# A new step table for a retention + FFN kernel: first group in half-tiles, dummy matmuls at the opening, weights no longer gated

## The chip, the cores and the metric

The kernel runs on one NeuronCore of a Trainium2 chip. The metric is the device time of one execution in microseconds (us). Thirteen executions of the kernel before are shown; one more execution of it was recorded by the hardware profiler, and every duration below is read from that record.

The core has a matmul engine (PE, with its weight loads listed apart as PEld), three engines for elementwise work (DVE, ACT, POOL), a queue engine (SP) that here only issues DMAs, and 16 DMA engines that move data between HBM and on-chip memory. Matmuls write to PSUM, eight banks of 128 x 512 float32. POOL does not touch PSUM in this kernel.

## The reference

```python
scores = q @ k.T / sqrt(64)                    # 8 batches, 8 heads, 576 positions, head width 64
Dmat   = where(rel >= 0, gamma[h] ** rel, 0)   # decay by distance, causal; gamma[h] = 1 - 2**(-5-h)
x      = (scores * Dmat) @ v                   # -> 4608 tokens x 512
h      = x @ w_in                              # 512 x 2048
g      = where(h > 0, h, exp(min(h, 0)) - 1)   # ELU
out    = g @ w_out                             # 2048 x 512, float32
```

Inputs and output are float32; the kernel multiplies in bfloat16.

## The kernel before

The work has two halves that run interleaved. **Attention** is cut into 40 *units*: five for each batch, of which four cover 256 positions of four heads (unit `u` has `T = (u % 5) // 2`, the 256 positions, and `w = u % 5 % 2`, the heads), and the fifth is a short tail of 64 positions and all heads. The decay is folded into q and k, so that a running state per head carries what lies before a chunk of 128 positions. **FFN** is cut into 9 *groups* of 512 tokens. Group 0 is batch 0's first 512 tokens, that is units 0 and 1 (tokens 0 to 255) and 2 and 3 (256 to 511). Group 1 holds unit 4 (the tail of batch 0, 64 tokens), units 5 and 6 (256 tokens), and three quarters of units 7 and 8.

Nothing is left to a scheduler. A string `PLAN` lists some 1550 steps; the kernel walks it once, each step emits its instructions, and every instruction is pinned, so each engine executes its own steps in exactly the order of the table and waits where data or a buffer is not there. The steps, with the line that their instructions carry in the profile:

- `ld.u.q/k/v` load 256 KB of float32 (L323; tails L319 and L315), issued on SP. Each DMA on SP waits for the completion of the one eight places before it. Nine buffers take q and k of a unit together (`rqk`), eight take v (`rv`), two take a tail's.
- `wi.n`, `wo.n` load a quarter of w_in or w_out with a cast to bfloat16 (L286; 1 MB read, 512 KB written), issued on POOL, in POOL's order.
- `ca.u.q/k/v.e` cast and scale q, k (L354, tails L350) or cast v (L211), on engine `e`: `v` is DVE, `s` ACT, `p` POOL. `tr` transposes four 128 x 128 pieces on PE (L374), `tc` copies them out of PSUM (L211); `dt` does the same by a DMA transpose on SP (L367).
- `st` state products, `sc` scores, `in` the part that comes from the running state, `va` scores times v, all on PE (L203, output names `x` and `sc`); `mk` applies the mask on DVE (L449, L452); `pm`, `pe` add up the state on DVE (L211, L536, L542); `dm`, `de` spread it into a block diagonal (L545); `ou` copies the result out of PSUM into the group's `xt` tile (L211).
- `f.g.ft.lo.n.nf.tag` is the first FFN product (L203, output `ph`): hidden tiles `ft` to `ft+nf-1` (128 hidden values each) of group `g`, tokens `lo` to `lo+n`, into PSUM bank `tag`. It needs quarter `ft // 4` of w_in. `ex` is the exponential on ACT (L585). Then either `re...s`, a relu in place on ACT (L591), or `re...v`, a subtraction of 1 on DVE that writes a tile called `em` (L594); `el` joins the two into `g` on DVE (L603 or L605).
- `a.g.it.m.tag` is a quarter `m` of the second product for 128 tokens (L203, output `pm`): it needs quarter `m` of w_out. `y` copies the sum out (L211), `so` stores it (L624, on POOL; the last four on SP).
- `wm.n.tag`: `n` matmuls of zeros, 128 x 512. The code is there and the table does not use it.

A step written `x>y` also waits until `y` has been completed: a *gate*. The table before has two: `wi.0>ld.2.v` and `ld.4.q>wo.1`.

The table before does units 0 to 3 first, then all sixteen hidden tiles of group 0 at 512 tokens, then the second product of group 0 with units 4 to 8 between its quarters, then group 1, whose first product is split into 320 tokens (units 4, 5, 6) and 192 tokens (units 7, 8). From group 2 on, first and second products of neighbouring groups alternate with attention between them.

Of the kernel before, what the change touches and what calls it, by code (L numbers as in the profile page):

```python
# [16 lines left out]
PAIRS = {('st', 0): ('pm', 'h2'), ('st', 1): ('pm', 'h2'), ('st', 2): ('pm', 'h2'), ('st', 3): ('h1', 'h2')}  # L17
STATE_PAIR = {0: ('st', 0), 1: ('st', 1), 2: ('st', 2), 3: ('st', 3)}
OUT_PAIR = {(3, 0): ('st', 3), (3, 1): 4, (4, 0): 6}
SCORE_PAIR = {4: 5}  # L20
PLAN = """
ld.0.q ld.0.k ld.0.v ld.1.q ld.1.k ld.1.v ca.0.q.v ld.2.q tr.0.q.h0 ld.2.k ca.0.k.p tc.0.q.v ld.2.v ca.0.v.s ld.3.q.0
tr.0.k.h1 tc.0.k.s ld.3.k.0 st.0 ca.1.q.v sc.0 ld.3.v.0 pm.0 mk.0 tr.1.q.h0 ld.3.q.1 dm.0.p ld.3.k.1 ca.1.k.p in.0
pe.0 ca.1.v.s ld.3.v.1 tc.1.q.v va.0 de.0.p ou.0.1.s tr.1.k.h1 ou.0.0.s ca.2.q.v st.1 tc.1.k.s pm.1 tr.2.q.h0 pe.1
dm.1.p sc.1 tc.2.q.v de.1.p mk.1 in.1 ca.2.v.s wi.0>ld.2.v ca.3.q.v.0 ca.2.k.p va.1 ca.3.v.s.0 ou.1.1.s ca.3.q.v.1
wi.1 ou.1.0.s tr.2.k.h1 st.2 tc.2.k.s ca.3.k.p.0 pm.2 ca.3.v.s.1 pe.2 ca.3.k.p.1 sc.2 tr.3.0.h0 mk.2 wi.2 st.3.0
st.3.1 tc.3.0.s dm.2.p tr.3.1.h0 pm.3 sc.3.0 va.2 de.2.p tc.3.1.s pe.3 mk.3.0 in.2 dm.3.p ou.2.0.s sc.3.1 va.3.0
mk.3.1 ou.2.1.s wi.3 in.3.0 in.3.1 ou.3.0.s.0 de.3.p ou.3.1.s.0 va.3.1 ou.3.1.s.1 wo.0 ou.3.0.s.1 f.0.0.0.512.1.h0
wo.1 f.0.1.0.512.1.h1 wo.2 ex.0.0.0 wo.3 re.0.0.0.v f.0.2.0.512.1.pm ex.0.1.0 el.0.0.0 re.0.1.0.s f.0.3.0.512.1.x0
ex.0.2.0 el.0.1.0 f.0.4.0.512.1.h2 ex.0.3.0 re.0.2.0.v re.0.3.0.s f.0.5.0.512.1.x1 el.0.2.0 ex.0.4.0 el.0.3.0  # L30
f.0.6.0.512.1.h0 ex.0.5.0 re.0.4.0.v re.0.5.0.s f.0.7.0.512.1.h1 el.0.4.0 ex.0.6.0 f.0.8.0.512.1.pm el.0.5.0 ex.0.7.0
re.0.6.0.v re.0.7.0.s f.0.9.0.512.1.x0 el.0.6.0 ex.0.8.0 f.0.10.0.512.1.h2 el.0.7.0 ex.0.9.0 re.0.8.0.v re.0.9.0.s
f.0.11.0.512.1.x1 ex.0.10.0 el.0.8.0 f.0.12.0.512.1.h0 ex.0.11.0 el.0.9.0 ld.4.q>wo.1 re.0.11.0.s f.0.13.0.512.1.h1
re.0.10.0.v ld.4.k ex.0.12.0 el.0.11.0 f.0.14.0.512.1.pm ld.4.v ex.0.13.0 el.0.10.0 re.0.13.0.s f.0.15.0.512.1.x0
re.0.12.0.v ld.5.q ex.0.14.0 el.0.13.0 a.0.1.0.h2 ld.5.k ex.0.15.0 el.0.12.0 ld.5.v ca.4.q.p re.0.15.0.s a.0.2.0.h1
re.0.14.0.v ld.6.q el.0.15.0 a.0.1.1 ld.6.k el.0.14.0 ca.4.k.p ld.6.v a.0.2.1 tr.4.q.h0 a.0.0.0.pm ld.7.q ca.4.v.p
tc.4.q.v a.0.1.2 a.0.0.1 ld.7.k ca.5.q.v a.0.2.2 ld.7.v ca.5.k.p tr.5.q.h0 a.0.0.2 tc.5.q.v ld.8.q ca.5.v.s tr.5.k.h0
a.0.1.3 ld.8.k ca.6.q.v tc.5.k.s tr.6.q.h0 ld.8.v y.0.1 ca.6.k.p sc.5 tc.6.q.v sc.4 st.5 mk.5 a.0.0.3 ld.9.q ca.6.v.s
so.0.1.p tr.6.k.h2 pm.5 ld.9.k y.0.0 a.0.2.3 mk.4 dm.5.p tc.6.k.s pe.5 ca.7.q.v a.0.3.0.pm ld.9.v so.0.0.p y.0.2
de.5.p in.5 ca.7.v.s in.4 ld.10.q ca.7.k.p sc.6 va.5 va.4 mk.6 st.6 ou.5.1.s tr.7.q.h0 a.0.3.1 so.0.2.p ou.5.0.s  # L40
ld.10.k ou.4.0.s pm.6 ou.4.1.s tc.7.q.v tr.7.k.h2 dm.6.p a.0.3.2 ca.8.q.v tc.7.k.s ld.10.v pe.6 ca.8.k.p tr.8.q.h1
in.6 tc.8.q.v va.6 ld.11.q a.0.3.3 ca.8.v.s de.6.p ou.6.1.s ou.6.0.s sc.7 st.7 y.0.3 mk.7 ld.11.k tr.8.k.h0 ca.9.q.p
f.1.0.0.320.1.h2 tc.8.k.s so.0.3.p ld.11.v f.1.1.0.320.1.h1 ex.1.0.0 pm.7 ca.9.k.p f.1.2.0.320.1.h0 pe.7 ld.12.q
ex.1.1.0 re.1.0.0.v dm.7.p re.1.1.0.s el.1.0.0 ex.1.2.0 ca.9.v.p dt.9 el.1.1.0 f.1.3.0.320.1.h2 de.7.p re.1.2.0.v
f.1.4.0.320.1.h1 ca.10.q.v ex.1.3.0 ca.10.k.p ld.12.k re.1.3.0.s el.1.2.0 ex.1.4.0 el.1.3.0 f.1.5.0.320.1.h0
re.1.4.0.v dt.10 ca.10.v.s f.1.6.0.320.1.h2 el.1.4.0 ex.1.5.0 a.1.0.0.pm ex.1.6.0 ca.11.q.v re.1.5.0.s ld.12.v
f.1.7.0.320.1.h1 re.1.6.0.v ld.13.q el.1.5.0 ca.11.k.p ex.1.7.0 el.1.6.0 f.1.8.0.320.1.h0 re.1.7.0.s ld.13.k
f.1.9.0.320.1.h2 ca.11.v.s el.1.7.0 ex.1.8.0 dt.11 f.1.10.0.320.1.h1 ca.12.q.v ex.1.9.0 a.1.0.1 re.1.8.0.v re.1.9.0.s
ex.1.10.0 el.1.8.0 ld.13.v in.7 el.1.9.0 ca.12.k.p sc.8 ld.14.q sc.9 re.1.10.0.v va.7 st.8 mk.8 ou.7.0.s
f.1.11.0.320.1.h0 ou.7.1.s f.1.12.0.320.1.h2 dt.12 ex.1.11.0 el.1.10.0 ca.12.v.s mk.9 f.1.13.0.320.1.h1 re.1.11.0.s  # L50
pm.8 ld.14.k ex.1.12.0 ca.13.q.v dm.8.p ex.1.13.0 ld.14.v el.1.11.0 re.1.13.0.s ca.13.k.p pe.8 f.1.14.0.320.1.h0
re.1.12.0.v el.1.13.0 ld.15.q a.1.0.2 ex.1.14.0 de.8.p el.1.12.0 re.1.14.0.v dt.13 f.1.15.0.320.1.h1 el.1.14.0
# [12 lines left out]
ca.19.q.p pm.15 ou.14.1.s f.2.0.0.512.1.h1 pe.15 dm.15.p ld.21.q f.2.1.0.512.1.h2 ca.19.k.p ex.2.0.0 ld.21.k de.15.p
re.2.0.0.v in.15 ex.2.1.0 sc.16 ca.19.v.p va.15 el.2.0.0 dt.19 st.16 re.2.1.0.s f.2.2.0.512.1.h0 mk.16 ou.15.0.s
ou.15.1.s f.2.3.0.512.1.h1 ld.21.v ca.20.q.p ex.2.2.0 pm.16 el.2.1.0 a.1.3.1 ld.22.q ex.2.3.0 dm.16.p pe.16 re.2.2.0.v
re.2.3.0.s ca.20.k.p f.2.4.0.512.1.h2 ld.22.k el.2.2.0 in.16 de.16.p el.2.3.0 ex.2.4.0 sc.17 va.16 ca.20.v.p st.17
mk.17 dt.20 ou.16.0.s f.2.5.0.512.1.h0 ou.16.1.s ca.21.q.p f.2.6.0.512.1.h1 re.2.4.0.v ex.2.5.0 ld.22.v pm.17
ca.21.k.p el.2.4.0 re.2.5.0.s a.1.3.2 ld.23.q ex.2.6.0 pe.17 ld.23.k el.2.5.0 dm.17.p f.2.7.0.512.1.h2 dt.21 de.17.p  # L70
re.2.6.0.v in.17 ca.21.v.p ex.2.7.0 el.2.6.0 sc.18 sc.19 va.17 ld.23.v st.18 ca.22.q.p re.2.7.0.s mk.18
f.2.8.0.512.1.h0 ou.17.1.s ld.24.q ou.17.0.s ca.22.k.p f.2.9.0.512.1.h1 mk.19 ex.2.8.0 pm.18 el.2.7.0 ld.24.k a.1.3.3
dm.18.p ex.2.9.0 re.2.8.0.v dt.22 ca.22.v.p re.2.9.0.s f.2.10.0.512.1.h2 pe.18 el.2.8.0 y.1.3 de.18.p el.2.9.0 ld.24.v
f.2.11.0.512.1.h0 ex.2.10.0 ca.23.q.p re.2.10.0.v in.18 in.19 ex.2.11.0 so.1.3.p ld.25.q sc.20 el.2.10.0 va.18
ca.23.k.p va.19 re.2.11.0.s st.20 mk.20 ld.25.k f.2.12.0.512.1.h1 ou.18.0.s ou.18.1.s ld.25.v ca.23.v.p
f.2.13.0.512.1.h2 ou.19.0.s pm.20 ou.19.1.s dt.23 el.2.11.0 ex.2.12.0 ca.24.q.p a.2.0.0.pm pe.20 ex.2.13.0 dm.20.p
re.2.12.0.v de.20.p ld.26.q re.2.13.0.s f.2.14.0.512.1.h0 el.2.12.0 ca.24.k.p el.2.13.0 f.2.15.0.512.1.h1 ex.2.14.0
dt.24 re.2.14.0.v f.3.0.0.512.1.h2 ex.2.15.0 ca.24.v.p el.2.14.0 re.2.15.0.s a.2.0.1 ld.26.k ca.25.q.p ex.3.0.0
el.2.15.0 f.3.1.0.512.1.h0 ld.26.v re.3.0.0.v ca.25.k.p ld.27.q f.3.2.0.512.1.h1 el.3.0.0 ex.3.1.0 ld.27.k ca.25.v.p
# [75 lines left out]
def kernel(  # L155
# [213 lines left out]
    def turn(u, part, tag):  # L369
        u = int(u)  # L370
        ptr[u, part] = p = psum[tag].tile([P, 4, P], BF16, name="ptr", tag=tag)
        for j in range(4):
            lo = (2 * j + int(part) if part in "01" else "qk".index(part) * 4 + j) * P
            last = pin(nc.tensor.transpose(p[:, j], flat(u)[:, lo : lo + P], ident))  # L374
# [33 lines left out]
    def state_pair(u):  # L408
        return STATE_PAIR.get(u, u)
# [266 lines left out]
```

## Time and profile before

| | us |
|---|---|
| median of 13 executions | 322.34 |
| lowest, highest | 320.97, 324.96 |
| the profiled execution, own time | 321.5 |
| its span, first to last instruction | 319.6 |

| engine | busy us | share of the span |
|---|---|---|
| PE | 297.6 | 93% |
| PEld | 154.6 | 48% |
| DVE | 208.4 | 65% |
| ACT | 181.8 | 57% |
| POOL | 146.2 | 46% |

A matmul counts as busy from its start until its result is out, about 0.38 us for 512 columns, while the next one starts 0.216 us after it (four in 0.86 us on the chain of waits): PE's busy share is therefore no share of its peak. In the lists, "x16" is a count, "mean ns" the mean length of one instruction, and "idle before" the time in which the engine stood still ahead of that group, with what ended the wait. "L203" and "L211" are helpers that many steps share, so the tile names tell them apart. The granted clock is the share of full speed that the throttle let PE have, as the record has it.

### The profile page before, as it was taken

To read this page: it belongs to the slowest core of one execution; us is meant where nothing else is said; L and a number is where in the kernel's file an instruction comes from. 1 tells how busy PE (TensorE), PEld (TensorE's weight loads), DVE (VectorE), ACT (ScalarE), POOL (GpSimd) and SP (SyncE) were. 2 spreads that over 40 slices of the span, in tenths; PEclk is the share of its full clock that TensorE was granted. 3 is DMA by queue.
4 is the path that set the end of the run, shared out by engine and by line. 5 is a ranking of instruction groups with operands and counts; after the bars stand their busy time and mean duration, and the time that the engine had idled before them with its cause. 6 is when DMAs were issued, how large, how long until landed. Compare 5 with 4: busy or idle time off the path is not lost.

```text
span 319.6 us, 7795 instructions
## 1 busy us (share of the span) xinstructions
PE 297.6 (93%) x3076; PEld 154.6 (48%) x3076; DVE 208.4 (65%) x387; ACT 181.8 (57%) x380; POOL 146.2 (46%) x223
## 2 busy tenths in 40 slices
PE   2799999598989899999999999999999999999995
PEld 1454355355745454454554555445544544444442
DVE  3959646979957998656868776777666654545400
ACT  3459526557637686556566656665666556465511
POOL 5790048515998877535566556654222020000000
PEclk9999999989999999999999999999999999999999
DMA  7999999999999999999999923322100100000022
GB/s 202 210 184 204 222 291 302 215 225 176 238 238 222 240 234 226 253 167 299 251 270 236 195 72 89 83 69 61 52 22 36 68 34 33 35 34 33 33 79 87
DMA packets 100085, 49.67 MB, mean 155 GB/s; under 512 B 44240, under 2 KB 97488, under 8 KB 100048
## 3 DMA queue, kind: packets, MB, share of 16 engines
q1 hardware_dynamic: 93264, 36.58, 56.0%
q0 software_dynamic: 6784, 12.59, 16.0%
q8 instruction: 24, 0.39, 0.5%
q14 instruction: 13, 0.11, 0.1%
HBM read 36.70 MB, written 9.44 MB: 144 GB/s over the span
## 4 chain that ended last, share of the span: by engine, by line
PE 80%; DMA 7%; DVE 4%; POOL 4%; ACT 2%; issue 1%; SPq 1%; ACTq 0%; DVEq 0%
PE pm L203 38%; PE ph L203 33%; PE x L203 6%; DMA w_out<-in_moe_w_out_dram 3%; PE sc L203 3%; DMA rqt<-in_k_dram 2%; DMA rv<-in_v_dram 2%; DVE em L594 1%; POOL qkn L354 1%; POOL w_in L286 1%; POOL s_mid L545 1%; PE ptr L374 1%; ACT xt L211 1%; DVE pt L449 1%; DVE qkn L354 1%
## 5 line engine op out<-in xcount | busy, mean ns | idle before, releaser
L203 PE MATMUL ph<-xt,w_in 128*128 128x512 bf16 (+2 forms) x640 | 145.0, 360 | 5.9 <-DVE g L605 4.1
L203 PE MATMUL pm<-w_out,g 128*128 128x512 bf16 x576 | 144.1, 380 | 0.0
L585 ACT ACTIVATE e<-ph 128x512 f32<-128x512 f32 (+2 forms) x152 | 87.1, 574 | 81.1 <-PE ph L203 77.1
L203 PEld LDWEIGHTS <-w_in 128*128 128x128 bf16 x640 | 61.4, 98 | 71.0 <-issue 8.3
L203 PEld LDWEIGHTS <-g 128*128 128x128 bf16 x576 | 54.6, 98 | 61.9 <-issue 0.7
L603 DVE SCALAR_TENSOR_TENSOR g<-e,ph 128x512 bf16<-128x512 f32 (+2 forms) x80 | 50.2, 631 | 36.6 <-ACT ph L591 35.3
L594 DVE TENSOR_SCALAR em<-e 128x512 bf16<-128x512 f32 (+2 forms) x76 | 42.4, 558 | 27.2 <-ACT e L585 27.1
L605 DVE SCALAR_TENSOR_TENSOR g<-ph,em 128x512 bf16<-128x512 f32 (+2 forms) x80 | 50.5, 635 | 2.8
L624 POOL DMA_DIRECT2D out_dram<-ot x32 | 18.4, 574 | 67.4 <-ACT ot L211 64.4
L449 DVE TENSOR_TENSOR pt<-sc,mask 128x1024 bf16<-128x1024 f32 x31 | 37.9, 1222 | 10.4 <-PE sc L203 9.9
L591 ACT ACTIVATE ph<-ph 128x512 f32<-128x512 f32 (+2 forms) x76 | 43.4, 571 | 0.0
L354 POOL TENSOR_TENSOR qkn<-rqk,gk 128x512 bf16<-128x512 f32 (+1 forms) x33 | 35.3, 1070 | 6.0 <-DMA rqk<-in_k_dram 5.9
L211 ACT CAST xt<-x 128x256 bf16<-128x256 f32 (+1 forms) x90 | 27.2, 393 | 15.8 <-PE x L203 15.3
L545 POOL TENSOR_TENSOR s_mid<-mid,diag 128x256 bf16<-128x256 f32 x32 | 20.1, 628 | 30.5 <-DVE mid L211 17.0
L211 ACT COPY ot<-pm 128x512 f32<-128x512 f32 x36 | 21.1, 586 | 19.8 <-PE pm L203 19.6
L354 POOL TENSOR_TENSOR qkn<-rqk,gq 128x512 bf16<-128x512 f32 x20 | 20.7, 1036 | 7.5 <-PE x L203 3.9
L211 POOL CAST vn<-rv 128x512 bf16<-128x512 f32 x20 | 12.7, 634 | 24.1 <-PE x L203 19.5
L545 POOL TENSOR_TENSOR s_end<-end,diag 128x256 bf16<-128x256 f32 x32 | 21.2, 662 | 0.3
L350 POOL TENSOR_TENSOR qkt<-rqt,gq 128x256 bf16<-128x256 f32 x16 | 9.7, 614 | 20.3 <-DMA rqt<-in_k_dram 19.2
L203 PE MATMUL x<-pt,vn 64*64 64x128 bf16 x512 | 13.9, 228 | 1.3 <-DVE pt L449 1.2
L203 PE MATMUL sc<-qkT 64*64 64x128 bf16 x512 | 14.5, 233 | 0.4 <-ACT qkT L211 0.3
L211 ACT CAST vn<-rv 128x512 bf16<-128x512 f32 (+1 forms) x13 | 7.6, 585 | 12.1 <-DMA rv<-in_v_dram 12.1
(54 smaller groups left out, 142.6 us busy)
## 6 DMA issues: line engine op xcount, KB each, us to landing
out_dram<-ot POOLq DMA_DIRECT2D x32, 256.0 KB, 3.8
rqk<-in_q_dram SPq DMA_DIRECT2D x31, 256.0 KB, 5.4
rqk<-in_k_dram SPq DMA_DIRECT2D x31, 256.0 KB, 5.5
rv<-in_v_dram SPq DMA_DIRECT2D x31, 256.0 KB, 5.3
w_in<-in_moe_w_in_dram POOLq DMA_DIRECT2D x4, 512.0 KB, 7.3
w_out<-in_moe_w_out_dram POOLq DMA_DIRECT2D x4, 512.0 KB, 12.0
rqt<-in_q_dram SPq DMA_DIRECT2D x8, 128.0 KB, 5.7
rqt<-in_k_dram SPq DMA_DIRECT2D x8, 128.0 KB, 4.9
```

The lines of the kernel that those rows point to most:

```text
L203: return pin(nc.tensor.matmul(*a, **kw))
L211: return pin(nc.scalar.copy(dst, src) if eng == "s" else engines[eng].tensor_copy(dst, src))
L350: return pin(engines[eng].tensor_tensor(dst[:, hs], src[:, hs], g, ALU.mult))
L354: return pin(engines[eng].tensor_tensor(dst[:, i, :, h0:h1], x, g, ALU.mult))
L449: return pin(nc.vector.tensor_tensor(ptt[u].rearrange("p i h n -> p (i h) n"), sc.rearrange("p i (h n) -> p (i h) n", h=2), m.to_broadcast ...
L545: return pin(engines[eng].tensor_tensor(dst.rearrange("p h (j d) -> p h j d", j=2), src.unsqueeze(2).to_broadcast([P, 2, 2, D]), diag.unsq ...
L585: return pin(nc.scalar.activation(e[:, : n * nf], ph[:, : n * nf], AF.Exp))
L591: return pin(nc.scalar.activation(ph[:, : n * nf], ph[:, : n * nf], AF.Relu))
L594: return pin(engines[eng].tensor_scalar_add(em[:, : n * nf], more[0][:, : n * nf], -1.0))
L603: last = pin(nc.vector.scalar_tensor_tensor(dst, more[0][:, c], -1.0, ph[:, c], ALU.add, ALU.min))
L605: last = pin(nc.vector.scalar_tensor_tensor(dst, ph[:, c], 0.0, more[1][:, c], ALU.max, ALU.min))
L624: return pin({"p": nc.gpsimd, "y": nc.sync}[eng].dma_start(out[i0 : i0 + P, :], ots.pop((int(g), int(it)))))
```

## The change

The edits in the code around the table are small. `xt` becomes flat, and for groups 0 and 1 it is laid out in segments (256 + 256 and 320 + 192 tokens), so that a copy into one segment and a matmul on the other touch different memory. Unit 3, which is loaded and cast in two halves, gets a layout in which each half is contiguous; the masked scores are stored half by half as well. A matmul of 512 tokens over two segments reads and writes with one more dimension.

```diff
-PAIRS = {..., ('st', 3): ('h1', 'h2')}
+PAIRS = {..., ('st', 3): ('h2', 'h1')}
+HALVED = (3,)
+SEGMENTS = {0: [(0, 256), (256, 256)], 1: [(0, 320), (320, 192)]}
...
-        return pin(engines[eng].tensor_tensor(dst[:, i, :, h0:h1], x, g, ALU.mult))
+        to = dst[:, i] if h is None else halved(dst)[:, int(h), i]
+        return pin(engines[eng].tensor_tensor(to, x, g, ALU.mult))
+    def halved(t):
+        return t.rearrange("p i e h d -> p (i e h d)").rearrange("p (g i e h d) -> p g i e h d", g=2, i=2, e=2, h=2)
...
-            xts[g] = xpool.tile([P, KJ, TG], BF16, name="xt", tag="xt")
+            xts[g] = xpool.tile([P, KJ * TG], BF16, name="xt", tag="xt")
+    def xt_part(g, lo, n):
+        a, m = segment(g, lo)
+        if lo + n > a + m:
+            return xt_tile(g).rearrange("p (a j n) -> p j a n", j=KJ, n=m)
+        return xt_tile(g)[:, KJ * a : KJ * (a + m)].rearrange("p (j n) -> p j n", j=KJ)[:, :, lo - a : lo - a + n]
...
             for j in range(KJ):
-                last = mm(ph[:, f * n : (f + 1) * n], w_sb["i"][(ft + f) // 4][:, j, c : c + P],
-                          xt[:, j, lo : lo + n], start=(j == 0), stop=(j == KJ - 1))
+                to = ph[:, f * n : (f + 1) * n]
+                if n > segment(g, lo)[1]:
+                    to = to.rearrange("p (a n) -> p a n", n=segment(g, lo)[1])
+                last = mm(to, w_sb["i"][(ft + f) // 4][:, j, c : c + P], xt[:, j], start=(j == 0), stop=(j == KJ - 1))
```

The bulk of the change is the table. Up to the start of group 4 it is a different order; from there on it has the same order, with other bank names. Its opening, old and new:

```diff
-ld.0.q ld.0.k ld.0.v ld.1.q ld.1.k ld.1.v ca.0.q.v ld.2.q tr.0.q.h0 ld.2.k ca.0.k.p tc.0.q.v ld.2.v ca.0.v.s ld.3.q.0
-tr.0.k.h1 tc.0.k.s ld.3.k.0 st.0 ca.1.q.v sc.0 ld.3.v.0 pm.0 mk.0 tr.1.q.h0 ld.3.q.1 dm.0.p ld.3.k.1 ca.1.k.p in.0
-pe.0 ca.1.v.s ld.3.v.1 tc.1.q.v va.0 de.0.p ou.0.1.s tr.1.k.h1 ou.0.0.s ca.2.q.v st.1 tc.1.k.s pm.1 tr.2.q.h0 pe.1
-dm.1.p sc.1 tc.2.q.v de.1.p mk.1 in.1 ca.2.v.s wi.0>ld.2.v ca.3.q.v.0 ca.2.k.p va.1 ca.3.v.s.0 ou.1.1.s ca.3.q.v.1
-wi.1 ou.1.0.s tr.2.k.h1 st.2 tc.2.k.s ca.3.k.p.0 pm.2 ca.3.v.s.1 pe.2 ca.3.k.p.1 sc.2 tr.3.0.h0 mk.2 wi.2 st.3.0
...
+ld.0.q ld.2.k ld.1.q ld.0.k ld.0.v ld.1.v ca.0.q.p ld.1.k ld.3.q.0 ca.2.k.v tr.0.q.pm wm.8.x0 ld.3.k.1 tc.0.q.s
+ld.3.q.1 ld.2.v ca.1.q.v tr.2.k.x1 ld.3.k.0 tr.1.q.pm wm.4.x0 ca.0.k.v ld.3.v.0 tc.1.q.s tc.2.k.v ld.3.v.1 wm.1.h0
+ca.0.v.v tr.0.k.pm ld.2.q tc.0.k.v ca.1.v.s ld.5.k st.0 sc.0 ld.5.q pm.0 wm.8.h0 ca.1.k.p pe.0 ld.6.q mk.0 ld.7.k
+dm.0.p ld.6.k ca.3.q.v.1 wi.0 tr.1.k.h1 st.1 ld.4.k tc.1.k.s va.0 pm.1 ca.2.v.p ld.4.q pe.1 de.1.v ca.3.q.p.0 st.2
+ld.5.v in.0 ca.3.k.v.1 ca.3.v.p.0 ca.3.v.s.1 sc.1 de.0.v ld.7.q ca.3.k.p.0 tr.3.1.h0 ou.0.0.v wm.7.h1 tc.3.1.s ld.6.v
+pm.2 dm.1.p mk.1 ou.0.1.s ld.4.v dm.2.p wi.1 ca.2.q.v tr.3.0.h0 in.1 ld.10.q tc.3.0.s wi.2 pe.2 tr.2.q.h1 ld.7.v va.1
+tc.2.q.v wi.3 ou.1.1.s ou.1.0.v ld.8.k st.3.1 sc.2 st.3.0 ld.8.q mk.2 f.0.2.0.256.2.h0 ca.5.k.p ld.9.q in.2 pm.3
+ld.9.k va.2 pe.3 wo.0 sc.3.0 ld.12.q f.0.0.0.256.2.pm ou.2.0.s mk.3.0 ex.0.2.0 dm.3.p ld.10.k ou.2.1.v va.3.0
+re.0.2.0.s sc.3.1 wo.1 ld.10.v in.3.0 mk.3.1 in.3.1 ex.0.0.0 ou.3.0.v.0 ou.3.1.s.0 el.0.2.0 va.3.1 f.0.4.0.256.2.h1
...
+a.0.1.0.h0 ca.4.k.p el.0.9.0 tr.6.k.x1 a.0.1.1 ca.5.v.p el.0.10.0 tc.6.k.s ca.7.k.p ca.4.q.v tr.6.q.x1 mk.5 ld.14.q
...
+re.1.8.0.s f.1.1.0.320.1.x1 y.0.2.v so.0.0.p f.1.4.0.320.1.h1 el.1.8.0 ex.1.1.0 ld.8.v ca.9.k.p f.1.3.0.320.1.h0
+re.1.1.0.s so.0.1.p f.1.0.0.320.1.x0 el.1.1.0 ex.1.3.0 dm.7.v a.0.3.1 ex.1.4.0 ca.9.q.p re.1.3.0.s ca.12.q.p ca.10.v.s
```

In words: the loads come in another order, and those of units 5, 6, 7 and 4 stand among or ahead of the weight loads; both gates are gone (three others, `ld.9.v>wi.3`, `ld.11.k>wo.2` and `ld.11.v>wo.0`, stand late in group 1). 28 dummy matmuls stand in five places of the opening. Hidden tiles 0 to 7 of group 0 are done in pairs for 256 tokens, the first two pairs before units 2 and 3 are finished; tiles 8 to 15 still take 512 tokens. Unit 8 is transposed by DMA instead of on PE. In groups 0 to 3 elementwise steps change engine: over the whole table `re` goes from 76 on ACT and 76 on DVE to 98 and 54, `ou` from 82 on ACT to 63 and 19 on DVE, `dm` and `de` from 64 on POOL to 52 and 12 on DVE, and six of the 36 `y` go to DVE.

## The prediction

> **What bounds the kernel now.** I read the page's slices first, then the busy times by stage, cut at the starts of group 0's first product (21.6), of the second product (35.7), of group 1 (56.5), its 192-token part (77.9), and groups 2, 3 and 4 (97.9, 120.9, 149.5).
>
> ```profile
> span 319.6 us, 7795 instructions
> PE   2799999598989899999999999999999999999995
> DMA  7999999999999999999999923322100100000022
> ```
> ```profile
> 0.00:21.60 21.60, 12.78 (x237) 8.66 (x237) 13.75 (x38) 10.00 (x22) 16.28 (x40) 1.00 0.95 199
> 21.60:35.70 14.10, 14.10 (x67) 6.35 (x65) 11.09 (x20) 12.18 (x24) 2.30 (x4) 1.00 1.23 202
> 35.70:56.50 20.80, 19.25 (x253) 10.31 (x252) 11.58 (x23) 9.09 (x20) 10.91 (x15) 1.00 1.17 284
> 56.50:77.90 21.40, 16.15 (x205) 9.97 (x202) 18.63 (x36) 12.39 (x33) 9.60 (x13) 0.92 1.06 198
> 77.90:97.90 20.00, 18.55 (x336) 12.90 (x329) 14.88 (x36) 11.03 (x29) 17.51 (x25) 1.00 1.21 237
> 97.90:120.90 23.00, 21.72 (x305) 11.42 (x304) 20.68 (x38) 16.35 (x38) 18.55 (x26) 1.00 1.25 225
> 120.90:149.50 28.60, 28.60 (x225) 13.65 (x224) 19.58 (x32) 17.08 (x34) 16.46 (x24) 1.00 1.09 237
> ```
>
> Columns: length, then PE, PEld, DVE, ACT, POOL busy, granted clock, DMA share, GB/s. From 121 on PE never stands, so what can be won lies before. In matmul pitch (0.863 for an `f` or `a` step of four 512-column matmuls, 0.54 for a 320-token step, 0.66 for a 192-token pair, 0.22 for a `tr`, 0.7 to 0.9 for a unit) the stages hold 5.2, 13.8, 18.2, 13.4, 17.7, 21.0 and 28.4 us of PE work. Lost: 16 in the opening, 3 beside the second product, 8 at the start of group 1, 2 each in the next two. The DMA engines are full to 180.
>
> Two more views are needed: the weight loads, and the timeline at three places.
>
> ```profile
> L286 POOL DMA_DIRECT2D w_in<-in_moe_w_in_dram x4: 803/807/942, 13.0 to 19.5; - x4
> DMA to landing us min/median/max: 5.5/7.3/8.2
> ```
> ```profile
> L286 POOL DMA_DIRECT2D w_out<-in_moe_w_out_dram x4: 747/765/803, 20.9 to 23.1; - x4
> DMA to landing us min/median/max: 9.4/12.0/15.0
> ```
> ```profile
> 4.70 0.61 PE L374 MATMUL ptr<-ident,qkn 128*128 128x128 bf16 x4 [4.70 <-DVE qkn L354]
> ...
> 32.74 0.72 SPq L319 DMA_DIRECT2D rqt<-in_q_dram  x1
> ...
> 39.52 1.18 POOL L350 TENSOR_TENSOR qkt<-rqt,gq 128x256 bf16<-128x256 f32 x2 [15.62 <-DMA rqt<-in_k_dram]
> ...
> 44.33 0.39 PE L374 MATMUL ptr<-ident,qkn 128*128 128x128 bf16 x4
> ...
> 58.05 2.68 DVE L594 TENSOR_SCALAR em<-e 128x320 bf16<-128x320 f32 x1
> ...
> 61.31 1.25 PE L203 MATMUL ph<-xt,w_in 128*128 128x320 bf16 x8 [2.99 <-DVE g L605]
> ```
>
> w_in lands from 18.5 to 27.7, w_out from 30.3 to 38.1, always ahead of PE. The tail's q, issued at 32.7, lands only after the last w_out at 38.1, 5.9 later: a load stands in line behind weights issued before it. Four transposes take 0.61 at first and 0.39 later: PE starts at half pitch (0.107 against 0.055 each). And `em`, 0.33 as a rule, took 2.68 beside POOL's operations and held PE for 2.99.
>
> **The opening.** 0.q lands at 3.8 as before, but `ca.0.q` is now on POOL, which is at its masks until 4.5 and takes 1.04 for it instead of DVE's 0.7: first transposes at 5.6 instead of 4.7. Then `wm.8`: eight at half pitch are 8 x 0.43 = 3.4 and hold PE to 9.5, with `tr.2.k` and `tr.1.q` queued behind; `wm.4` and `wm.1` cost 1.1 (warm) to 2.1. 0.k is now the fourth load, not the second (7.6 instead of 4.7), and `tr.0.k` shares bank `pm` with `tr.1.q`, so it follows that copy-out, at 11.5 to 12.5. After its copy, `st.0` and `sc.0` stand at 12.2 to 13.9; the trace before has 7.35 and 7.84. `wi.0`, behind `pm.0` and `dm.0`, is issued at 13.6 to 15.0 (12.95 before), `wi.1` to `wi.3` from 18.0 to 21.3 (14.9 to 19.5 before). Following the table with row durations (`mk` 1.23, `tc` 0.42 to 0.58, `ou` 0.45), units 0 and 1 are in `xt` at 20.6 to 22.2. The warmed PE returns some 0.6 per unit, which is inside these bounds. So the dummies bring no net gain here: what they warm waits for data that comes later.
>
> As a page has it, the Trainium skill, "TensorE: Matmul & The Clock Gate", Part 1, gives half rate until some 3.4 us of sustained activity. By it one block of dummies would do; the 0.61 against 0.39 agrees, and the sum is the same either way.
>
> **The weights.** This is where I expect the loss. Removing the gates lets the loads of units 5, 6, 7 and 4 take the line first. A load costs 0.89 (256 KB at 296 GB/s between 5 and 12), a weight quarter 2.6 to 2.8 (512 KB written at 205 GB/s between 24 and 34). Units 0 to 3 are in by 14.6. Ahead of `wi.0` stand five or six loads and one or both halves of unit 4: 4.9 to 6.2; it lands at 22.1 to 23.8 and the first `f` starts there, not at 21.6. `wi.1` follows three or four more transfers: 27 to 29.7. Ahead of `wi.3` stand in all 9 to 12 loads and unit 4, 9.2 to 11.8, and four quarters: 34.5 to 38.0, middle 36.4 (27.7 before). PE is in order: `f.0.4` waits for `wi.1` with all else behind it, `f.0.12` for `wi.3`; seven `f` steps, `sc.5` and an `a` step (7.2) remain, so group 0's first product ends at 43.6 instead of 35.5. w_out follows at 39 to 48 and `wo.3`, which POOL issues after `dm.5`, at 54, just in time.
>
> For a weight behind loads the trace has no row. The nearest is a store among loads, up to 6.8 to landing against 2.0 at the least, so I take the line as one in both directions; if the queues share, the case is the first rival's. The skill's "DMA: Bandwidth & Descriptors", Queues, rings and completion order, speaks against a line: each engine goes round its queues. The 5.9 of the tail's q, which had to outwait every weight, does not look so. By the rule `wi.1` would come some 3 us earlier, but `wi.3`, with as many bytes moved by then, within 1 us of the same time, and the sum would stay.
>
> **From there to group 4**, counting steps of the new table: largest engine's sum, times what the trace before shows of length over largest sum in that stage.
> - To group 1: PE 11 `a` (9.5), 5 `tr` (1.1), units 4 to 7 (2.3) = 12.9; before 21.0 for 18.2, ratio 1.15: 14.7. Group 1 starts at 58.3 (56.5 before), with four `a` steps (3.5) fewer done.
> - 320-token part: `re` is now on ACT 14 times of 15: 30 x 0.44 + casts, copies 3.4 = 16.6; DVE 14.4 with one `em`, so the 2.68 and its kind go; PE 15.9 with 6 `a`. ACT is late next. 21.4 over 18.6 was 1.15: 19.0, and PE loses 3 instead of 8.
> - 192-token part: DVE 11 `el` (7.0), `mk` (4.3), `pm`/`pe` (2.0), casts, copies, spreads (4.4) = 17.7, POOL down to 8.4; ratio 1.07: 19.0.
> - Group 2: PE 22.6, DVE 23.2 (14 `el` at 0.69, `mk` 5.5, the rest 8); 23.0 over 21.7: 24.6. Group 3: PE 16 `f`, 16 `a`, two units = 29.3, fully used: 29.5.
>
> Sum: 43.6 + 14.7 + 19.0 + 19.0 + 24.6 + 29.5 = 150.4 for group 4's start, against 149.5: 0.9 later. From there the order is the same: 0. Flat `xt`, segments, half layouts and the other bank names move the same bytes and columns: 0, and if an `f` over two segments were slower, eight steps show it. Two `tr` fewer are 0.4, counted. The profiled execution, 321.5, would become 322.4; it lies 0.8 under the median, so 323.2.
>
> Bounds: with all ratios 1 and `wi.3` at 34.5, 41.7 + 99.7 = 141.4, or 8.1 less: 314.2. With `wi.3` at 38.0, ratios 1.24 (21.4 over the 17.3 that DVE's steps take undisturbed) in the 320-token part and 1.1 to 1.25 elsewhere, 45.2 + 112.8 = 158.0: 330.8.
>
> **Rivals.** *The weights do not wait* (they land 5.5 to 8.2 after issue, as before): then the first product runs from 22 to 38.5, and group 4 starts at 145.3: 4.2 less, 318.1. For it: there is no row against it; against it: the tail's 5.9. *The later stages run at their largest sum* (99.7 instead of 106.8): 7.1 less, 316.1. For it: one `em` in the 320-token part; against it: no stage before group 3 did it. *Slower: SP's line.* `ld.14.q` waits for a tail buffer that `ca.4.q` frees at 46; behind it on SP stand `dt.8`, 8.v, `dt.9`, 11.q, `dt.10`, and so `ca.11` and `dt.11`; `ca.9.q` on POOL in turn stands behind the stores of group 0. A DMA transpose lands 4.6 after issue, at most 8.0. `dt.9` is issued at about 61.5 and `sc.9` wanted at 67: above 5.5 it decides, and `sc.9`, `sc.11` and `sc.12` each lose 2 to 3, with all of PE behind: 7 more, 330.
>
> **Numbers.** The summed case 0.50 (its own range 319.5 to 327: 0.05 faster, 0.22 same, 0.23 slower), free weights 0.14, full stages 0.12, SP's line 0.24. Faster by over 0.5% (about what can be told from no change, 1.6 us) 0.31, within 0.22, slower 0.47. The range 316 to 331 leaves out most of the full stages' lower half and the worst of SP's line.
>
> **What would show it.** `sc` first at 12 to 14; first `ph` at 22 to 24 with idle PE ended by w_in; last w_in landing at 34 to 38; group 1 at 58, group 4 at 150. It is wrong if `ph` never waits for w_in, if w_in's time to landing stays under 9, or if `sc` stands still for `qkT` of a DMA transpose for over 3 in all.

## The result and the profile after

The kernel after takes 331.6 us (median of 11 executions, 326.9 to 334.1) where the kernel before, run beside it, takes 322.1. Four of the eleven, 332.1 to 334.1, count as slow executions, and the ratios of this document are of the others alone: after takes 1.0246 times as long as before (95% interval 1.0211 to 1.0280), which makes 330.0 us. The profiled execution of after took 329.6 us, with a span of 327.9. The predicted 323.2 is 8.4 us under the median and 6.8 under the 330.0; the predicted range, 316 to 331, holds the second figure and misses the first by 0.6.

In what follows TensorE is PE, VectorE DVE, ScalarE ACT and GpSimd POOL; line numbers of after are a few higher than those of before. First the page's slices of after (2.5% of the span each), then the busy times by stage, with the columns of the prediction's table. The cuts are the starts of group 0's first product, the end of that product (43.7), and the starts of group 1, of its 192-token part, and of groups 2, 3 and 4.

```profile
span 327.9 us, 7881 instructions
PE   2877997999998699998999999999999999999995
PEclk9999999999999979999999999999999999999999
DMA  7999997289997799999899992322200001000012
```
```profile
0.00:23.15 23.15, 14.04 (x208) 7.98 (x209) 13.55 (x40) 6.55 (x13) 14.07 (x36) 1.00 1.03 243
23.15:43.70 20.55, 17.81 (x181) 11.59 (x182) 16.72 (x37) 14.16 (x29) 8.74 (x11) 1.00 1.21 217
43.70:59.30 15.60, 13.48 (x202) 7.16 (x201) 12.39 (x24) 5.50 (x11) 4.53 (x6) 1.00 0.82 166
59.30:77.00 17.70, 16.97 (x213) 10.38 (x212) 16.09 (x32) 13.82 (x39) 10.50 (x15) 1.00 0.68 166
77.00:94.10 17.10, 16.86 (x322) 12.00 (x322) 15.27 (x41) 9.51 (x24) 7.92 (x12) 1.00 1.20 224
94.10:124.50 30.40, 25.58 (x310) 12.07 (x309) 24.01 (x46) 17.39 (x35) 14.97 (x18) 0.94 0.94 208
124.50:156.10 31.60, 30.03 (x234) 13.87 (x233) 23.05 (x39) 20.01 (x40) 15.34 (x22) 1.00 1.19 243
```

After reaches group 2 at 94.1, 3.8 us ahead of before (97.9), with three `a` steps (2.6 us of PE) fewer done. Group 1 took 34.8 us instead of 41.4, and PE stood 1.0 us in it instead of 6.7. Then group 2 takes 30.4 instead of 23.0 and group 3 31.6 instead of 28.6; from group 4 on it is 171.8 against 170.1. In group 2 no engine is full: PE stands 4.8 us, and a slice shows a lower clock (0.94 over the stage, 1.8 us of work). The waits of that stage, longest first (total, times, longest), and three places of the timeline show who is late:

```profile
ACT e L611 <- PE ph L205: 7.5, 8, 1.2
POOL qkn L357 <- DMA rqk<-in_k_dram: 6.5, 2, 3.4
POOL qkt L352 <- DMA rqt<-in_q_dram: 6.0, 1, 6.0
```
```profile
99.19 0.63 SPq L321 DMA_DIRECT2D rqt<-in_q_dram  x1
...
103.42 0.61 POOL L352 TENSOR_TENSOR qkt<-rqt,gq 128x256 bf16<-128x256 f32 x1 [5.96 <-DMA rqt<-in_q_dram]
...
115.41 0.29 PE L205 MATMUL x<-qkT,s_end 128*128 128x128 bf16 x2 [2.37 <-POOL s_end L556]
...
116.50 3.21 PE L205 MATMUL ph<-xt,w_in 128*128 128x512 bf16 x8
```

The casts wait for their loads. Unit 19's q is issued at 99.19 and lands at 103.35, POOL stands 6.0 us for it with the casts of 17 and 18 behind. Later PE stands 2.37 us for a spread (`de`) that POOL does after unit 20's k, again a cast that waited for its load, and the next eight products take 3.21 us (1.89 at the full clock). The feeding of the units, read load by load (us; cast is the end of the last cast of q and k):

| unit | ld.k issued, before / after | cast, before / after | dt issued, before / after |
|---|---|---|---|
| 14 | 71.0 / 71.0 | 77.4 / 78.1 | 79.2 / 82.2 |
| 15 | 76.9 / 79.3 | 83.2 / 87.4 | 84.4 / 87.4 |
| 16 | 78.6 / 89.4 | 88.3 / 96.7 | 89.5 / 96.7 |
| 17 | 83.2 / 86.8 | 92.1 / 105.0 | 95.6 / 105.1 |
| 18 | 87.9 / 92.9 | 96.4 / 108.1 | 99.6 / 110.5 |

The rows of unit 16's k, its load and its cast, in before and then in after:

```profile
78.61 0.51 SPq L323 DMA_DIRECT2D rqk<-in_k_dram  x1
...
87.25 1.03 POOL L354 TENSOR_TENSOR qkn<-rqk,gk 128x512 bf16<-128x512 f32 x1
```
```profile
89.43 1.50 SPq L325 DMA_DIRECT2D rqk<-in_k_dram  x1
...
95.11 1.59 POOL L357 TENSOR_TENSOR qkn<-rqk,gk 128x512 bf16<-128x512 f32 x1 [3.19 <-issue]
```

When group 2 begins, before has cast unit 18; after, 3.8 us earlier, is casting unit 16. It has run ahead with group 1's products and fallen behind with the units.

### The profile page after: what moved, and what is told of

Read it like the earlier page. It is cut to its first block, busy times and chain, and to the rows that moved or that the text cites. A ratio compares the mean times of both kernels' runs of the same rounds, so it can differ in the third digit from the quotient of the medians.

```text
span 327.9 us, 7881 instructions
## 1 busy us (share of the span) xinstructions
PE 301.9 (92%) x3128; PEld 156.3 (48%) x3128; DVE 222.3 (68%) x423; ACT 180.4 (55%) x375; POOL 131.4 (40%) x198
## 3 DMA queue, kind: packets, MB, share of 16 engines
q0 software_dynamic: 6784, 12.59, 14.7%
## 4 chain that ended last, share of the span: by engine, by line
PE 55%; DMA 13%; DVE 9%; POOL 7%; issue 7%; SPq 6%; ACT 1%; POOLq 0%; ACTq 0%; DVEq 0%
PE pm L205 27%; PE ph L205 22%; DMA w_in<-in_moe_w_in_dram 4%; POOL qkn L357 3%; PE x L205 3%; DMA rqk<-in_k_dram 3%; SPq L325 3%; DMA rvt<-in_v_dram 2%; PE sc L205 2%; DMA rqt<-in_k_dram 2%; DMA out_dram<-ot 2%; DVE g L629 2%; SPq L373 1%; DVE qkn L357 1%; PE warm L205 1%
## 5 line engine op out<-in xcount | busy, mean ns | idle before, releaser
L205 PE MATMUL ph<-xt,w_in 128*128 128x512 bf16 (+3 forms) x672 | 145.8, 351 | 4.6 <-DMA w_in<-in_moe_w_in_dram 2.7
L611 ACT ACTIVATE e<-ph 128x512 f32<-128x512 f32 (+2 forms) x152 | 87.0, 575 | 83.2 <-PE ph L205 78.7
L629 DVE SCALAR_TENSOR_TENSOR g<-e,ph 128x512 bf16<-128x512 f32 (+3 forms) x112 | 63.0, 580 | 41.1 <-ACT ph L617 40.2
L617 ACT ACTIVATE ph<-ph 128x512 f32<-128x512 f32 (+2 forms) x98 | 54.3, 561 | 0.0
L620 DVE TENSOR_SCALAR em<-e 128x512 bf16<-128x512 f32 (+1 forms) x54 | 31.3, 580 | 18.1 <-ACT e L611 18.1
L631 DVE SCALAR_TENSOR_TENSOR g<-ph,em 128x512 bf16<-128x512 f32 (+2 forms) x56 | 37.1, 666 | 2.0
L357 POOL TENSOR_TENSOR qkn<-rqk,gk 128x512 bf16<-128x512 f32 (+1 forms) x25 | 27.0, 1080 | 20.2 <-DMA rqk<-in_k_dram 17.0
L357 POOL TENSOR_TENSOR qkn<-rqk,gq 128x512 bf16<-128x512 f32 (+1 forms) x24 | 25.8, 1078 | 7.6 <-PE x L205 3.9
L213 POOL CAST vn<-rv 128x512 bf16<-128x512 f32 (+1 forms) x19 | 11.9, 625 | 16.0 <-PE x L205 11.7
L213 ACT COPY qkT<-ptr 128x512 bf16<-128x512 bf16 x11 | 6.4, 587 | 17.1 <-PE ptr L380 17.1
L380 PE MATMUL ptr<-ident,qkn 128*128 128x128 bf16 x56 | 6.0, 240 | 7.5 <-POOL qkn L357 6.3
```

The lines of the kernel that those rows point to most:

```text
L205: return pin(nc.tensor.matmul(*a, **kw))
L213: return pin(nc.scalar.copy(dst, src) if eng == "s" else engines[eng].tensor_copy(dst, src))
L357: return pin(engines[eng].tensor_tensor(to, x, g, ALU.mult))
L611: return pin(nc.scalar.activation(e[:, : n * nf], ph[:, : n * nf], AF.Exp))
L617: return pin(nc.scalar.activation(ph[:, : n * nf], ph[:, : n * nf], AF.Relu))
L620: return pin(engines[eng].tensor_scalar_add(em[:, : n * nf], more[0][:, : n * nf], -1.0))
```

## The experiments

Ratios are to the kernel before, run beside them on the same chip; after is 1.0246. The order of the runs is that in which the questions came up.

**Layouts, or order?** The table of before in the code of after.

```diff
-PLAN = <table of after>
+PLAN = <table of before, gates included>
```


> The code of after (segmented xt tiles, unit 3 by halves, pt with the halves outside) with the whole step table of before, gates included, so that only the layouts are changed. All theories that put the loss into the order: within 1.5 us of before's 322. If the layouts cost something (the strided moving operand of 512 tokens of groups 0 and 1, the masked product with one more dimension): 325 or more.

Measured: 322.2 us, ratio 1.0013 (0.9988 to 1.0038). The layouts cost nothing; all of the loss is in the order of the steps.

**One wait in group 2.** The three loads that stood behind `dt.16`, put ahead of it.

```diff
-... dt.16 ld.17.v ld.19.q ld.18.q ...      (order on SP)
+... ld.17.v ld.19.q ld.18.q dt.16 ...
```


> The kernel after, with one step moved: dt.16 goes behind ld.17.v, ld.19.q and ld.18.q on SP. In the trace of after dt.16 left SP at 96.73 and these three loads followed at 98.56, 99.19 and 99.86; GpSimd stood 6.0 us for ld.19.q (landed 103.35). Theory 1 (SP's line: loads stand behind transposes that wait): the three loads go at 94.8 to 96.7, GpSimd's 6.0 us wait shrinks below 2, group 2 falls from 30.4 to 25 to 28 us, the time from 331.6 to 326 to 329. Theory 2 (the casts' order on GpSimd and VectorE holds group 2, not the loads): the wait only moves to the next cast, group 2 stays above 29.5 and the time within 1 us of 331.6.

Measured: 327.4 us, ratio 1.0144 (1.0102 to 1.0186), clear of after's interval. Moving one step on SP is worth about 3.3 us, theory 1's number. Its mechanism is shown in part only: in the profiled execution (at a lower clock than after's) group 2 takes 26.7 us (first exponential to first exponential) instead of 30.4, but POOL still stands 4.9 us for unit 19's q, where under 2 was expected.

**The same, everywhere.** 38 loads moved ahead of transposes.

```diff
+ before each dt.u: every ld whose cast stands ahead of the second next dt
```


> The kernel after, with 38 loads moved on SP alone: a load whose cast stands ahead of the second next DMA transpose is issued before the present one, so that no load of units 8 and up stands behind a transpose that waits for a later cast. Theory 1 (SP's line): GpSimd's waits for rqk (17.0 us), rvt (7.3) and rqt (6.0) fall to a third in sum, group 2 takes 24 to 26 us and group 3 29 to 30, the whole 322 to 326. Theory 2 (casts' order): the waits pass to other releasers, the whole stays above 329. Theory 3 (DMA itself is short: the earlier loads delay weights or transposes): the last w_out lands later than 55.2 or the transposes land over 6 us after issue, and the whole is above 331.

Measured: ratio 1.0190 (1.0144 to 1.0236): 6 us over before, within the interval no better than moving one step. None of the three theories has its number. In its profiled execution (at a lower clock than after's, so lengths are not compared) POOL's waits for loads between 45 and 160 us are down to 5.4 of 21.9 us, as theory 1 said, but `dt.15`, with six more loads ahead of it, is issued at 94.2 instead of 87.4, and PE stands 8.7 us for transposes. What the casts gain, the transposes lose: SP has hardly a free place there.

**Where is the loss made?** Two orders can be spliced at the start of a group, with the steps that are left at that point taken in the other table's order. Three such runs, with the ones above, split the table into opening with group 0, group 1, and the rest:

```diff
-PLAN = <after>
+PLAN = <after up to the first f.2> + <what is left, in the order of before>     e3
+PLAN = <before up to the first f.2> + <what is left, in the order of after>     e9
+PLAN = <after up to the first f.1> + <what is left, in the order of before>     e10
```


> The order of after up to its first product of group 2 (94.1 us in its trace), and the order of before for all that is then left. Theory 1 and theory 2 (the loss is made by the order of steps in groups 2 and 3): before took 221.7 us from its group 2 to the end, with 3.0 us less work of TensorE left at that point, so the span is 94.1 + 3.0 + 221.7 = 319 and the time about 321, up to 324 with the change of order itself. Rival (group 2 inherits the loss: units, casts and loads that lag at 94 us, whatever order follows): 327 or more.

> The order of before up to its first product of group 2 (97.9 us in its trace), and the order of after for all that is then left: the mirror of the run that followed after with before (331.3). Theory P (what the units have behind them when group 2 starts decides: before has cast units 17 and 18 by then, after unit 16): 321 to 324. Theory Q (the order of after in groups 2 and 3 loses by itself, whatever stands ready): 327 or more. Between: both have a share.

> The order of after up to its first product of group 1 (59.3 us in its trace), and the order of before for all that is then left. The first exponential of group 1 came at 60.0 in after and at 57.3 in before. Theory R (the opening costs what it is late, and the order of group 1 in after lets the units fall behind): 322 + 2.7 = 324.7, from 323.5 to 326.5. Theory S (the units are behind already at 59 us, since the loads, the casts of units 9 to 12 and both queues are as after left them): 329 or more.

| opening, group 0 | group 1 | from group 2 on | ratio (95%) |
|---|---|---|---|
| before | before | before (after's code) | 1.0013 (0.9988 to 1.0038) |
| after | before | before | 1.0074 (1.0037 to 1.0110) |
| before | before | after | 1.0102 (1.0039 to 1.0165) |
| after | after | before | 1.0292 (1.0230 to 1.0354) |
| after | after | after | 1.0246 (1.0211 to 1.0280) |

The opening and group 0 cost 0.74%, 2.4 us, as theory R had it. With before's order behind it, group 1's order costs 1.0292 - 1.0074, or 7.0 us, though group 1 itself is the stage that after does faster. The rest in after's order costs 3.3 us on the state that before leaves and nothing that can be seen on after's own: between theories P and Q. So what was 321 in the expectation of the first splice became 331: the lag is in the state at group 2, and before's order can't make it good. There PE stands 8.6 us for one step (the profile's groups between 94 and 125, then rows of POOL, of the splice after/after/before):

```profile
L207 PE MATMUL x<-qkT,s_mid 128*128 128x128 bf16 x6 | 0.9, 246 | 8.6 <-POOL s_mid L558 8.6
```
```profile
104.12 0.61 POOL L215 CAST vn<-rv 128x512 bf16<-128x512 f32 x1 [3.46 <-DMA rv<-in_v_dram]
...
108.99 0.62 POOL L558 TENSOR_TENSOR s_mid<-mid,diag 128x256 bf16<-128x256 f32 x1
```

The spread that PE waits for (`dm.15`) stands in before's order on POOL behind the casts of units 17 and 18; POOL stood 3.46 us for the load of unit 17's v, issued at 99.7. PE's granted clock was then 0.67 from 106 to 118 us, and 0.973 to 0.983 over the four executions of this splice, so a part of the 7.0 us is a lower clock behind the stop.

The shares do not simply add: 7.0 us is the price of group 1's order where before's order follows. After's opening, before's group 1 and after's rest were not run together. If the opening's 0.74% is added to 1.0102, group 1's order costs some 2.3 us where after's own order follows (an estimate). What is shown is that after's opening and group 0 cost 2.4 us by themselves, and that the order from group 1 on makes up the other 5.5 of after's 7.9; how these divide between group 1's order and the rest depends on which is put back first.

In the splice after/before/before unit 16's k is issued at 81.1 and units 16, 17 and 18 are cast by 90.7, 94.5 and 98.8, within 2.4 us of before's. Group 2 (first exponential to first exponential) then takes 23.0 us; before has 23.2, after 30.4, and the splice after/after/before 32.4. In the splice before/before/after units 16 to 19 are cast within 0.5 us of before's times, but units 21 and 22 late again: their q and k are cast by 117.0 and 133.1, where before has 108.9 and 112.8 and after 123.0 and 137.4. So the rest in after's order puts these two late by itself.

**Which stop in group 1?** In after, POOL stands 8.1 us at 53.4 for a store of group 0, with the casts of units 9, 12 and 10 behind it, behind these `dt.9` on SP (8.6 us), and behind that the loads of 13 and 11.

```diff
-... so.0.0.p ca.9.k.p ... so.0.1.p ca.9.q.p ca.12.q.p ... ca.10.k.p ...     (order on POOL)
+... ca.9.k.p ... ca.9.q.p ca.12.q.p ... ca.10.k.p so.0.0.p so.0.1.p ...
```


> The kernel after, with two stores moved on GpSimd alone: so.0.0.p and so.0.1.p go behind ca.10.k.p. In the trace of after GpSimd stood 8.1 us (53.42 to 61.55) for the first of them, whose tile was copied at 60.6; behind it stood the casts of units 9, 12 and 10 (their loads landed at 47.6 to 50.1), behind those dt.9 on SP (8.6 us), and behind dt.9 the loads of units 13 and 11 (65.25 on). Theory A (this stop is where the lag of group 2 begins): dt.9 goes at 55 to 57 instead of 64.0, the loads of 13 and 11 about 8 us sooner, group 2 takes 25 to 27 us instead of 30.4, and the time is 325 to 328. Theory B (the lag is made later, by loads and transposes that follow each other on SP from 78 us on): the first loads come sooner, but the masked products of units 16 to 21 come when they came, and the time stays within 1.5 us of 331.6.

Measured: ratio 1.0283 (1.0205 to 1.0360): theory A fails. `dt.9` did go at 55.7 and group 2 shrank to 26.4 us (first exponentials 98.5 to 125.0), but group 3 begins when it began in after: unit 21's casts of q and k end at 124.8 (123.0 in after), and group 3 takes 34.9 (31.6 in after). The time is the one that theory B gave, and the masked products of units 16 to 21 come within 2.6 us of after's. And the casts that now run at 53.6 to 55.7 run beside DVE's cast of unit 4's v (DVE and PE lines of the timeline of this run, then the same two steps in after):

```profile
50.99 4.89 DVE L216 CAST vt<-rvt 128x256 bf16<-128x256 f32 x1
...
55.94 0.33 PE L208 MATMUL x<-ptt,vt 64*64 64x64 bf16 x8 [4.25 <-DVE vt L216]
```
```profile
50.81 2.76 DVE L213 CAST vt<-rvt 128x256 bf16<-128x256 f32 x1
...
53.63 0.26 PE L205 MATMUL x<-ptt,vt 64*64 64x64 bf16 x8 [2.12 <-DVE vt L213]
```

2.1 us more of PE's standing are paid for the earlier casts; and this execution had a lower clock in two slices before 60 us, so that its group 1 began 3.8 us late.

**Both stops filled.** The same two stores, nine loads put into the time in which SP stood for `dt.8` and `dt.9`, and the move of the three loads.

```diff
-... dt.8 ld.8.v dt.9 ld.13.q ld.11.q dt.10 ld.11.k ld.9.v ld.11.v ld.12.k ld.14.k ld.13.k ...     (order on SP)
+... ld.8.v ld.13.q ld.11.q ld.11.k dt.8 ld.9.v ld.12.k ld.14.k ld.11.v ld.13.k dt.9 dt.10 ...
```


> The kernel after with both stores moved as in the run before, nine loads (8.v, 13.q, 11.q, 11.k ahead of dt.8, 9.v, 12.k, 14.k, 11.v, 13.k ahead of dt.9) put into the time in which SP stood for dt.8 and dt.9 (9.5 and 8.6 us), and dt.16 behind ld.17.v, ld.19.q and ld.18.q. Theory A: the two stops and the wait of 6.0 us for ld.19.q go together; group 2 at 24 to 25 us, the time 321 to 325. Theory B: the time is that of the run with dt.16 alone moved, 326 to 328. Theory C (the casts of units 11 to 17 on GpSimd and VectorE wait for their turn, not for data): within 1.5 us of 331.6.

Measured: ratio 1.0261 (1.0192 to 1.0330): after's time, theory C's number. The loads of q and k of 11 to 13 land by 63.9 at the latest, up to 15 us sooner, and their casts end at 77.5, 80.2 and 82.0 (74.2, 76.9 and 78.6 in after). They wait for their turn among group 1's steps, and here too group 1 begins late, by 4.4 us, behind the same cast of 4.89 us on DVE. `ld.15.q`, behind `dt.11` and `dt.12`, goes at 81.5 (78.2 in after). Counted from group 1's first exponential, unit 16 is cast after 35.2 us here, 34.6 in the run before, 36.7 in after and 31.0 in before: the two stops are at most 2 of the 5.7 us by which it is late. Group 2 does shrink, to 25.7 us. What the filled stops would bring without the slower cast of unit 4's v was not run.

**The dummies.**

```diff
-wm.8.x0 wm.4.x0 wm.1.h0 wm.8.h0 wm.7.h1
```


> The kernel after without its 28 dummy products (8.5 us of TensorE in the trace, all of it ahead of the first product with w_in). The prediction put them at no net gain: the time stays within 1 us of 331.6. If they bought the full clock for the opening, the scores of unit 0 and the first product of group 0 come 1 us or more later and the time grows by as much; if they stood in the way (3.6 us cold at 6.67 to 10.3 ahead of the transposes of unit 0), they come 1 us or more sooner.

Measured: 328.5 us, ratio 1.0175 (1.0100 to 1.0250). The interval just overlaps after's, so the gain of 2.3 us is likely, not certain. In its profile the scores of unit 0 stand at 9.99 (13.14 in after), `wi.0` is issued at 11.95 (14.30), and group 0's first product starts at 21.07 (23.15). About 0.5 us of each may be no gain: after's profile has its first transposes at 6.27, this one at 5.72. The dummies did buy speed: four transposes in a row take 0.58 to 0.61 us here all through the opening, and 0.39 to 0.40 in after from 12.11 on. But those directly behind the first eight dummies still started 0.105 us apart, as at first, and real work had stood behind 3.6 us of dummies.

**The weights.**

```diff
-dm.0.p ld.6.k ca.3.q.v.1 wi.0 tr.1.k.h1 ... dm.1.p ... dm.2.p wi.1
+wi.0 wi.1 dm.0.p ld.6.k ca.3.q.v.1 tr.1.k.h1 ... dm.1.p ... dm.2.p
```


> The kernel after with wi.0 and wi.1 issued on GpSimd ahead of dm.0.p, in the 2.3 us in which it stood there: at about 11.5 and 12.3 instead of 14.30 and 20.21. By the line of DMA in which loads and weights are served in the order of issue they land at 17 to 20 and 20 to 24 instead of 23.10 and 29.15, and TensorE's idle 0.43 + 1.89 us for w_in is gone: group 1 starts 2 us sooner, at 57. Theory A or B (the feeding of units sets groups 2 and 3, not TensorE's start): the later stages give it back, the time gains at most 1 us. Rival (the chain runs through TensorE from the weights on): the gain of 2 us reaches the end, 329 to 330.

Measured: 326.1 us, ratio 1.0109 (1.0078 to 1.0141): 4.4 us less than after. The quarters land at 20.2, 23.9, 27.5 and 31.1 (23.1, 29.2, 32.7 and 36.3 in after), PE never stands for w_in, and the first exponential of group 1 comes at 57.6 instead of 60.0. Both expectations were too small. What reaches the end is more than PE's 2.4 us at group 1: `dt.16` goes at 93.1, not 96.7, and group 2 takes 25.8 us instead of 30.4. Which casts gained by it was not taken apart.

**The parts together.** The two weights first, no dummies, `dt.16` behind the three loads, and `ca.4.v` and `re.1.0.0` on ACT.

```diff
-ca.4.v.v  re.1.0.0.v
+ca.4.v.s  re.1.0.0.s      (and the edits of the three runs)
```


> The kernel after with wi.0 and wi.1 ahead of dm.0.p (alone it measured 5.5 us), without dummy products (alone 3.1 us), with dt.16 behind three loads (alone 4.2 us), and with ca.4.v and the side piece re.1.0.0 on ScalarE instead of VectorE (there the two took 2.76 and 2.15 us beside GpSimd's work, and TensorE stood 2.1 us for the first). If the parts add: 331.6 - 5.5 - 3.1 - 4.2 - 2 = 317. If they are shares of the same waits: 323 to 326, the best of them alone less a little.

Measured: ratio 1.0115 (1.0076 to 1.0155), the same as with the weights alone. (The expectation's 5.5, 3.1 and 4.2 are differences of medians; by the ratios the three are 4.4, 2.3 and 3.3 us.) The parts do not add; that they are shares of the same waits fits this. One of them shows how a removed wait uncovers the next: with the tail's cast out of the way PE stands for the last quarter of w_out instead.

```profile
54.46 1.89 PE L207 MATMUL pm<-w_out,g 128*128 128x512 bf16 x7 [2.77 <-DMA w_out<-in_moe_w_out_dram]
```

**One step of before.** The piece of 2.68 us that the prediction showed.

```diff
-re.1.0.0.v
+re.1.0.0.s      (in the table of before)
```


> The kernel before with one step changed: re.1.0.0 on ScalarE (a relu in place) instead of VectorE (em). In the trace of before this em took 2.68 us at 58.05, beside GpSimd's casts, where the next ones of its shape took 0.3 to 0.9, and TensorE stood 2.99 and 0.95 us for the joins behind it, and then ran at a granted clock of 0.91 from 60 to 80 us (1.8 us of work). If the stretched piece is the cause: 317.5 to 320. If GpSimd only stretches whichever operation of VectorE comes next: within 1 us of 322.

Measured: ratio 0.9992 (0.9957 to 1.0027), no gain. The slow piece is there again, one step on, and PE stands for its join:

```profile
60.03 2.31 DVE L596 TENSOR_SCALAR em<-e 128x320 bf16<-128x320 f32 x1
...
63.40 2.19 PE L205 MATMUL ph<-xt,w_in 128*128 128x320 bf16 x8 [2.38 <-DVE g L607]
```

No run was faster than before.

## Why the prediction was right or wrong

**The opening** went as worked out: `sc.0` at 13.1 (12.2 to 13.9), `wi.0` issued at 14.3 (13.6 to 15.0), first product at 23.15 (22 to 24). The dummies' price, set at nothing, is more likely 2 us against them.

**The weights** landed in each of the three ranges, and group 0's first product ended at 43.7 (43.6 predicted). The reason given, one line for loads and weights, does not hold here, so these numbers came out right in part by luck. With both weights first, the landings from 26.6 on are load 26.6, weight 27.5, load 30.2, weight 31.1, load 33.6, weight 34.4, load 36.9, weight 38.0: the loads (256 KB, the last two 128 KB) and the weight quarters land in turn, some 3.5 us a pair. `wi.2`, issued at 18.6, lands ahead of unit 6's k, issued at 13.6. The packets of that run between 31.0 and 34.5 us (queue 0 has the weights, queue 1 the loads: packets, MB, share of 16 engines) show how:

```profile
q0 software_dynamic: 506, 0.50, 84.6%
q1 hardware_dynamic: 508, 0.24, 35.4%
```

The two queues move packet for packet, and since a packet of the weights is some 1 KB and one of the loads some 0.5 KB, a quarter (512 KB) and a load (256 KB) are about as many packets each. The rule that the prediction set aside (the Trainium skill, "DMA: Bandwidth & Descriptors", Queues, rings and completion order: each DMA engine goes round the queues that have work) fits these rows. It does not explain the tail's q in before, on which the prediction rested: from its issue at 32.74 until 36.0 the profile counts 674 packets of the weights' queue and not one of the loads'. Why is open.

**Group 1** held: 59.3, 77.0 and 94.1 against 58.3, 77.3 and 96.3. That ACT would be late next, and PE lose 3 us in the 320-token part, did not come: PE lost 0.7. In the stretch before it PE stood 2.1 us for unit 4's v, a cast that the new table puts on DVE beside POOL's casts (2.76 us); the prediction had let that kind of piece go. (12.9 times 21.0 over 18.2 is 14.9, not 14.7; nothing hangs on the 0.2.)

**The step that failed is group 2's term**: 23.2 of the largest engine times 1.06, 24.6, measured 30.4. The ratio was read from a stage of before into which the units came two ahead. The sum counted how much work each engine had left, and not how far loads, casts and transposes had come at the boundary; a chain of load, cast, transpose and scores does not show in any engine's busy time. That the order from group 1 on is where the time goes is shown by the splices (5.5 of the 7.9 us); that the lag of the units at group 2 is what costs there is shown with before's order behind it (7.0 us), and for after's own order it is argued from the waits of its trace. Group 3 (29.5, measured 31.6) and "from there 0" (1.7) have smaller shares, group 2's earlier start gives 2.2 back: 5.8 + 2.1 + 1.7 - 2.2 = 7.4, less 0.2 for rounding and for the time around the span. The other 1.2 us of the 8.4 is that after's profiled execution lies 2.0 under its median, before's 0.8.

**The rivals.** Weights that do not wait: no, w_in took 8.8 to 14.5 to land (5.5 to 8.2 in before) and PE stood 2.7 for it. Stages at their largest sum: no. SP's line, at 330 with 0.24, gave nearly the measured time, and it is this rival that carries the range up to 331. The kind of cause was right, but not its place, so the number is luck. SP did stand 6.1 and 8.6 us for `dt.8` and `dt.9` (53.44 and 64.01, behind loads that were issued by 47.32 and 55.41; the 9.5 in the expectation of the two filled stops is not in these rows); `dt.9` landed at 66.4, under the bound of 5.5 after 61.5, and the scores of 9, 11 and 12 lost nothing. The two runs that undid this stop gained nothing, though both began group 1 some 4 us late behind a slower cast, so a smaller share of it is not ruled out. The units that were late are 16 to 22, some 35 us later. The test named for it, scores that stand over 3 us for transposes, showed 1.5: PE stood for states and casts instead, so the test was on the wrong row.

**Layouts 0**: right, 1.0013.

**What stays open.** Which steps of group 1's order make the lag is not isolated. The trace suggests the SP line from 79 to 90: after puts unit 15's k at 79.3 and unit 16's at 89.4, with two transposes of 13 and 14, three loads of v and `dt.15` between (81.1 in the splice with before's group 1), and the casts of 11 to 13 behind the products of group 1. Moving loads alone gave from 3.3 us to nothing; casts and transposes moved with them were not tried apart from the whole order.

## What to carry to other kernels

When an order makes one stage shorter, ask what it has put off: at the stage's end compare, unit by unit, how far loads, casts and transposes are, and price the next stage with that lead, not with engine sums alone. Splicing two orders at stage boundaries tells in a few runs which part of a long table costs what; here it pointed at what the stage that had become faster left behind. The shares so found need not add, since an order also fits the state for which it was made: run all combinations before a share is given to one part. Gains measured one at a time (4.4, 3.3 and 2.3 us here) need not add either: together, with one edit more, they gave 4.2.

## What the runs showed of the hardware

DVE's tail cast of 128x256 takes 0.28 us at 112.30 in after, with POOL at rest, 2.76 beside POOL's casts and 4.89 when three more of POOL's casts stand beside it: it ends about when POOL's row of operations ends. In before, taking the slow piece away from DVE made the next one slow (2.68 becomes 2.31, one step on); with the parts together, where both pieces went to ACT, none of the pieces left on DVE between 46 and 66 us was stretched like that. The Trainium skill, "GPSIMD Engine Reference", Specifications, says that GpSimd shares its memory interfaces with VectorE and that some kinds of VectorE instructions contend; these rows agree with the sharing and give the size. Whether this cast and this subtraction are of the kinds that the page names, no run here shows.

Executions of one kernel differ in part by the granted clock: of after's, the one at 1.000 took 326.9 us, those between 0.982 and 0.984 took 331.6 to 332.1. It is not the whole of it, since two at 0.989 and 0.990 took 333.4 and 334.1. A stall can cost twice: PE's 2.37 us at 113 were followed by 3.21 us for 1.89 us of products, at a granted clock of 0.57 from 116.5 to 119.7. It need not: with the parts together PE stood 2.77 us at 54, and no slice of that profile shows a lower clock.
